# Gated linear attention feeding a cosine-gated MLP: the attention output made as token rows and transposed by TensorE or by a DMA, in a new order of units

## The chip, the core and the metric

The kernel runs on one core of a Trainium2 chip. The metric is the device time of one execution in microseconds (us). The engines are named as in the profile: PE is TensorE's matmuls, PEld its weight loads, DVE is VectorE, ACT is ScalarE, POOL is GpSimd, and SP issues the DMAs. A time is the median of a kernel's runs. A span is what one profiled execution shows from its first to its last instruction, and is 1 to 2 us shorter. PSUM is the memory that PE writes its results to.

## The reference

```python
# q, k, v, alpha: [4, 8, 768, 48];  w_in: [384, 2048];  w_out: [2048, 384]
for t in range(S):                                   # attention with a decaying state
    state = alpha[:, :, t, :, None] * state + einsum('bhd,bhe->bhde', k[:, :, t], v[:, :, t])
    y[:, :, t] = einsum('bhd,bhde->bhe', q[:, :, t], state)
x = y.transpose(0, 2, 1, 3).reshape(B * S, H * D)    # 3072 tokens x 384
h = x @ w_in
out = (h * cos(h)) @ w_out
```

## The kernel before

The 3072 tokens go through in 24 chunks of 128. One chunk passes through small units, and each unit has a letter. A string of letters with chunk numbers is the program: each engine executes its units in the order of that string, without looking ahead to a later unit. These units matter here:

| unit | engine | what it does | PSUM it writes |
|---|---|---|---|
| T, then t | PE, then DVE | transposes k and q; t copies them out | g |
| S, then u | PE, then DVE and POOL | the chunk's addition to the state; u adds and scales (DVE's part is called sc) | g |
| A, then m | PE, then DVE | scores; m masks them out of PSUM | big |
| Y, then y | PE, then DVE | attention output; y copies it out | g |
| F, f, p | PE, ACT, DVE | first half of the hidden layer, its cosine, the gating product | big |
| G, g, q | PE, ACT, DVE | the same for the second half | big |
| V and W, then e | PE, then ACT | the two halves of the second matrix; e copies the sum out | o |
| C, N, l, E | PE and ACT | cumulative log decay of two chunks, every second step; needs another ACT table | big |

PSUM pool g has **one** buffer, used by T, S and Y in turn. Each of them must wait until DVE has emptied the one before. So does o, which has one buffer too; big has three.

```python
    def outputs(j):                       # unit Y, before: 128x64 halves of the array
        t = ps.tile([C, 512], FP, tag="g")          # ps = tile_pool(bufs=1)
        # ... mms: per half 10 matmuls (6 of them in a batch's first chunk)
        kt, start, stop, lhsT, rhs = mms[half][i]   # lhsT: 64 columns of v or of the state
        nc.tensor.matmul(t[64 * half : 64 * half + 64, kt * C : (kt + 1) * C],
                         lhsT, rhs, start=start, stop=stop, skip_group_check=True)

    def ev_outputs(j):                    # unit y, before: what it copies is x already transposed
        t = work.tile([C, 3, C], BF, tag="xT")
        nc.vector.tensor_copy(out=t.rearrange("r k t -> r (k t)"), in_=y_ps.pop(j)[:, 0 : 3 * C])
        x_t[j] = t                        # F(j) and G(j) read it

    run(START)                            # the first chunks, in an order of their own
    for s in range(S0, NCH + 2):          # S0 = 4, NCH = 24
        # ... g = (s + 3) // 2; odd = s % 2 == 1; V = s - 2
        run(f"a{s + 7} k{s + 4} v{s + 4}")          # loads
        run(f"o{s + 2} T{s + 1} t{s + 1} F{s} f{s} S{s + 1} u{s + 1} A{s + 1} m{s + 1}")
        run(f"V{V} G{s} g{s} p{s} Y{s + 1} y{s + 1} q{s}")
        if odd: run(f"N{g} l{g + 1}")
        run(f"W{V} e{V}")
        if odd: run(f"C{g} E{g}")
```

## Time and profile before

| | before |
|---|---|
| time | 209.12 us (2 runs, 209.04 and 209.20) |
| PE busy / DVE / ACT / POOL | 95% / 66% / 63% / 38% |
| PE's share of the chain that ended last | 82% |
| one chunk in the steady part | 7.1 us, 7.6 us with C |
| first T of chunk 5 / of chunk 23 / end of the span | 54.1 / 185.8 / 208.2 us |

The timeline of the kernel before on PE, one step. The columns are start and duration in us, then the source line, what it computes, and how many; a bracket at the end would give idle time before the row. L210 is T, L323 is F or G, L249 is S, L227 is A, L347 is V or W, and L304 is Y, of which only the first and the last row are shown:

```profile
127.51 0.38 PE L210 MATMUL t<-ident_bf,khb 128*128 128x128 bf16 x4
127.73 0.39 PE L210 MATMUL t<-ident_bf,qhb 128*128 128x128 bf16 x4
127.96 1.50 PE L323 MATMUL t<-t,w_114 128*128 128x128 bf16 x24
129.30 0.33 PE L249 MATMUL t<-vpb,khb 128*128 128x96 bf16 x4
129.56 0.40 PE L227 MATMUL t<-t 48*128 48x128 bf16 x8
129.89 1.47 PE L347 MATMUL o_new<-w_116,g_new 128*128 128x384 bf16 x8
131.20 1.50 PE L323 MATMUL t<-t,w_114 128*128 128x128 bf16 x24
132.64 0.25 PE L304 MATMUL t<-t,ub 128*64 128x128 bf16 x2
...
133.11 0.28 PE L304 MATMUL t<-t,vpb 128*64 128x128 bf16 x4
133.32 1.47 PE L347 MATMUL o_new<-w_116,g_new 128*128 128x384 bf16 x8
134.63 0.39 PE L210 MATMUL t<-ident_bf,khb 128*128 128x128 bf16 x4
```

There is no bracket: PE never waits. Between the three users of g lie other units. F (1.34 us) separates T from S; A, V and G (3.1 us) separate S from Y; W (1.31 us) separates Y from the next T. DVE empties g in that time. Y itself takes from 132.64 to 133.32, 0.68 us.

### The profile page before, as it was taken

To read this page: it belongs to the slowest core of one execution; us is meant where nothing else is said; L and a number is where in the kernel's file an instruction comes from. 1 tells how busy PE (TensorE), PEld (TensorE's weight loads), DVE (VectorE), ACT (ScalarE), POOL (GpSimd) and SP (SyncE) were. 2 spreads that over 40 slices of the span, in tenths; PEclk is the share of its full clock that TensorE was granted. 3 is DMA by queue.
4 is the path that set the end of the run, shared out by engine and by line. 5 is a ranking of instruction groups with operands and counts; after the bars stand their busy time and mean duration, and the time that the engine had idled before them with its cause. 6 is when DMAs were issued, how large, how long until landed. Compare 5 with 4: busy or idle time off the path is not lost.

```text
span 208.2 us, 6187 instructions
## 1 busy us (share of the span) xinstructions
PE 196.8 (95%) x2645; PEld 149.0 (72%) x2647; DVE 136.7 (66%) x163; ACT 130.4 (63%) x142; POOL 79.6 (38%) x124
## 2 busy tenths in 40 slices
PE   7996869899999999999999999999999999999982
PEld 2343558677787887877878787787878878787851
DVE  7106857799776668487686685766776776777320
ACT  2064594998964955955937839739659558434420
POOL 3005362485570371561730931912804617401000
PEclk9999997999999999999999999999999999999999
DMA  6999999999999377566765955874774461101112
GB/s 139 312 197 319 186 218 360 260 179 199 179 225 191 80 151 157 113 148 123 160 131 93 188 117 106 162 152 97 135 154 94 100 114 43 41 2 39 38 38 77
DMA packets 106204, 30.29 MB, mean 145 GB/s; under 512 B 100288, under 2 KB 105408, under 8 KB 106176
## 3 DMA queue, kind: packets, MB, share of 16 engines
q1 hardware_dynamic: 106176, 29.89, 66.6%
q8 instruction: 20, 0.33, 0.7%
q14 instruction: 8, 0.07, 0.1%
HBM read 25.17 MB, written 4.72 MB: 144 GB/s over the span
## 4 chain that ended last, share of the span: by engine, by line
PE 82%; DVE 6%; DMA 4%; issue 4%; POOL 1%; SPq 1%; ACT 0%; POOLq 0%; DVEq 0%; ACTq 0%
PE o_new L347 32%; PE t L323 29%; PE t L304 8%; PE t L210 5%; DMA t<-in_k_dram 4%; PE t L227 3%; PE t L249 2%; PE cum_new L161 1%; DVE w_114 L121 1%; DVE g_new L338 1%; DVE t L216 1%; DVE qhb L193 1%; PE cum_new L165 1%; DVE t L309 1%; DVE t L236 1%
## 5 line engine op out<-in xcount | busy, mean ns | idle before, releaser
L331 ACT ACTIVATE c_sb<-t,halfpi 128x1024 bf16<-128x1024 f32 x48 | 53.3, 1115 | 41.7 <-PE t L323 41.3
L323 PE MATMUL t<-t,w_114 128*128 128x128 bf16 x1152 | 72.6, 220 | 0.4 <-DVE g_new L338 0.4
L347 PE MATMUL o_new<-w_116,g_new 128*128 128x384 bf16 x384 | 70.2, 327 | 0.6 <-ACT o_sb L363 0.6
L323 PEld LDWEIGHTS <-w_114 128*128 128x128 bf16 x1152 | 67.9, 99 | 3.5 <-issue 0.5
L338 DVE TENSOR_TENSOR g_new<-t,c_sb 128x1024 bf16<-128x1024 f32 x48 | 58.4, 1219 | 15.2 <-ACT c_sb L331 14.7
L191 POOL TENSOR_TENSOR khb<-t,icp_new 128x384 bf16<-128x384 f32 x24 | 25.0, 1041 | 74.8 <-ACT icp_new L179 73.7
L347 PEld LDWEIGHTS <-g_new 128*128 128x128 bf16 x384 | 34.1, 98 | 24.2 <-issue 0.8
L263 POOL TENSOR_TENSOR ub<-sc,Em 128x384 bf16<-128x384 f32 x20 | 17.4, 870 | 33.1 <-DVE sc L261 33.1
L236 DVE TENSOR_TENSOR t<-t,mask_f 128x1024 bf16<-128x1024 f32 x24 | 29.2, 1215 | 0.0
L193 POOL TENSOR_TENSOR qhb<-t,cp_new 128x384 bf16<-128x384 f32 x22 | 22.0, 1000 | 0.0
L216 DVE COPY t<-t 128x1024 bf16<-128x1024 bf16 x24 | 16.5, 687 | 8.1 <-PE t L210 8.1
L309 DVE CAST t<-t 128x384 bf16<-128x384 f32 x24 | 13.3, 554 | 11.4 <-PE t L304 11.3
L363 ACT ACTIVATE o_sb<-o_new 128x384 f32<-128x384 f32 x22 | 10.7, 485 | 15.9 <-PE o_new L347 15.8
L261 DVE TENSOR_TENSOR sc<-t,ub 128x384 f32<-128x384 f32 x20 | 11.1, 557 | 13.8 <-PE t L249 13.8
L370 PE MATMUL w_ps<-warm 128*128 128x512 bf16 x61 | 17.3, 435 | 1.4 <-DVE warm L56 1.2
L331 ACT ACT_TABLE_LOAD x13 | 16.7, 1283 | 0.2
L141 ACT ACT_TABLE_LOAD x13 | 16.7, 1283 | 0.2
L304 PE MATMUL t<-t,vpb 128*64 128x128 bf16 x288 | 15.9, 222 | 0.2 <-DVE t L216 0.2
L179 ACT ACTIVATE icp_new<-cum_new 128x768 f32<-128x768 f32 (+1 forms) x13 | 9.8, 757 | 7.3 <-PE cum_new L165 7.3
L370 PEld LDWEIGHTS <-warm 128*128 128x128 bf16 x63 | 6.5, 109 | 10.4 <-issue 4.5
L304 PE MATMUL t<-t,ub 128*64 128x128 bf16 x160 | 13.0, 227 | 1.0 <-DVE t L216 0.8
L304 PEld LDWEIGHTS <-vpb 128*64 128x64 bf16 x288 | 13.1, 111 | 0.9 <-issue 0.4
(47 smaller groups left out, 152.9 us busy)
## 6 DMA issues: line engine op xcount, KB each, us to landing
a_new<-in_alpha_dram SPq DMA_DIRECT2D x24, 192.0 KB, 3.7
t<-in_v_dram SPq DMA_DIRECT2D x24, 192.0 KB, 4.3
t<-in_k_dram SPq DMA_DIRECT2D x24, 192.0 KB, 4.0
t<-in_q_dram SPq DMA_DIRECT2D x24, 192.0 KB, 4.3
out_dram<-o_sb SPq DMA_DIRECT2D x24, 192.0 KB, 2.0
w1f<-in_moe_w_in_dram SPq DMA_DIRECT2D x2, 1536.0 KB, 7.8
w2f<-in_moe_w_out_dram SPq DMA_DIRECT2D x2, 1536.0 KB, 10.3
```

Source lines behind the costliest of these rows:

```text
L141: nc.scalar.preload_act_table_set("natural_log_exp_and_others")
L191: nc.gpsimd.tensor_tensor(out=khb[:, j % 3, :, 0:D], in0=k_sb, in1=icp.rearrange("s (h d) -> s h d", h=H), op=ALU.mult)
L193: qeng.tensor_tensor(out=qhb[:, j % 3, :, 0:D], in0=q_sb, in1=cp[:, 0:HD].rearrange("s (h d) -> s h d", h=H), op=ALU.mult)
L216: nc.vector.tensor_copy(out=t, in_=qkT_ps.pop(j))
L236: nc.vector.tensor_tensor(out=t.rearrange("s (h t) -> s h t", h=H), in0=A_ps.pop(j).rearrange("s (h t) -> s h t", h=H), in1=mask_f.unsquee ...
L263: eng.tensor_tensor(out=ub[:, j % 3, :, 0:96].rearrange("r p (a e) -> r p a e", a=2), in0=sc.rearrange("r p (a e) -> r p a e", a=2), in1=E ...
L304: nc.tensor.matmul(t[64 * half : 64 * half + 64, kt * C : (kt + 1) * C], lhsT, rhs, start=start, stop=stop, skip_group_check=True)
L323: nc.tensor.matmul(t[:, f], w1[:, kk, ft * C : (ft + 1) * C], x_t[j][:, kk], start=(kk == 0), stop=(kk == 2))
L331: nc.scalar.activation(out=c_sb, in_=h_ps[j, half], func=AF.Sin, bias=halfpi, scale=1.0)
L338: nc.vector.tensor_tensor(out=g_t[j][:, half * HF : (half + 1) * HF], in0=h_ps.pop((j, half)), in1=c_t.pop((j, half)), op=ALU.mult)
L347: nc.tensor.matmul(o_ps[j][:, 0:DM], g_t[j][:, ft], w2[:, ft], start=(f == 0 and (half == 0 or not whole)), stop=(f == HF - 1 and (half == ...
L370: nc.tensor.matmul(w_ps, warm[:, 0:C], warm, start=True, stop=True)
```

## The change

Its intent: Y's products use only 64 columns of the array at a time. With the scores as the stationary operand instead, the output comes out as 128 token rows, and the streamed operand is 48 or 96 columns long, so PE has less to do. The price is that x must then be transposed. Five first chunks do that on PE, the later ones by one DMA each. The units are put in a new order, apparently to leave the DMA time: V and W now lie between Y and F.

```diff
-    VS = 112
+    JD = 5
-    vpb = consts.tile([C, 3, H, VS], BF, tag="vpb")
-    nc.vector.memset(vpb, 0.0)
-    ub = consts.tile([C, 3, NP, C], BF, tag="ub")
+    vpb = consts.tile([C, 3, H, D], BF, tag="vpb")
+    ub = consts.tile([C, 3, NP, 96], BF, tag="ub")
@@ def outputs(j):   (the 20 half-width matmuls are cut)
+        for p in range(NP):
             if not first:
+                nc.tensor.matmul(t[:, p * 96 : (p + 1) * 96], qT[:, (NP + p) * C : (NP + p + 1) * C],
+                                 ub[:, (j - 1) % 3, p], start=True, stop=False, skip_group_check=True)
+            for h in (2 * p, 2 * p + 1):
+                nc.tensor.matmul(t[:, h * D : (h + 1) * D], A_t[j][:, ACOL[h] * C : (ACOL[h] + 1) * C],
+                                 vpb[:, j % 3, h], start=first, stop=True, skip_group_check=True)
@@ def ev_outputs(j):   (the old lines, and the bookkeeping of y_t and x_t, are cut)
+        t = work.tile([C, HD], BF, tag="y_sb")
+        nc.vector.tensor_copy(out=t, in_=y_ps.pop(j)[:, 0:HD])
+        if j >= JD:
+            x = work.tile([C, 3, C], BF, tag="xT", bufs=3)
+            nc.sync.dma_start_transpose(out=x, in_=y_t.pop(j))
+        else:
+            t = ps.tile([C, 3, C], BF, tag="g")
+            for kt in range(3):
+                nc.tensor.transpose(t[:, kt], y_t[j][:, kt * C : (kt + 1) * C], ident_bf)
+            x = work.tile([C, 3, C], BF, tag="xT", bufs=3)
+            nc.vector.tensor_copy(out=x, in_=t)
@@ main loop
-        run(f"o{s + 2} T{s + 1} t{s + 1} F{s} f{s} S{s + 1} u{s + 1} A{s + 1} m{s + 1}")
-        run(f"V{V} G{s} g{s} p{s} Y{s + 1} y{s + 1} q{s}")
-        if odd: run(f"N{g} l{g + 1}")
-        run(f"W{V} e{V}")
-        if odd: run(f"C{g} E{g}")
+        run(f"o{s + 2} T{s + 1} t{s + 1} S{s + 1} u{s + 1} V{V} A{s + 1} m{s + 1} W{V} e{V}")
+        run(f"F{s} f{s} p{s} G{s} g{s} Y{s + 1} y{s + 1} q{s}")
+        if odd: run(f"N{g} l{g + 1} C{g} E{g}")
```

## The prediction

> **What bounds the kernel now.** TensorE. The page gives PE 95% busy, DVE 66%, ACT 63%; the chain of waits is 82% PE. In the timeline of 125 to 140 us PE never stops: one chunk takes 7.1 us, or 7.6 us with the cumulative sums. Its order is T (transposes) 0.45, F (first half of the hidden layer) 1.34, S (state) 0.27, A (scores) 0.33, V 1.31, G 1.4, Y (attention output) 0.68, W 1.31.
>
> The order matters because T, S and Y all write the one PSUM bank "g" (pool of one buffer), which DVE must empty in between. Now each emptying is covered: F lies between T and S, A V G between S and Y, W between Y and T.
>
> **What the change removes.** Y had 20 half-width matmuls in 0.68 us, plus 0.09 us of drain before them (timeline). Afterwards it is 4 matmuls of 96 columns and 8 of 48: an estimate of 0.41 us from the 43 ns that a 96-column matmul of S takes and some 30 ns for a short one. That is some 8 us in all, all of it on PE.
>
> **What it adds and moves.** The new order on PE is T S V A W F G Y (C). Now nothing lies between T and S, nor (but 0.5 us of sums) between Y and the next T. So PE waits for DVE twice per chunk. DVE's order is t, sc, mask, gate p, y, gate q. y stands behind p, which stands behind ACT's cosine f, which stands behind F: a closed loop. From y's start, with the timeline's durations: y 0.55, so T issues at 0.6 and completes at 1.2; t must wait for q (0.46 to 1.59) and ends at 2.27; S issues at 2.33, V ends at 3.8, A at 4.14, W at 5.45, F at 6.8 (complete 6.95); f 7.0 to 8.1; p 8.15 to 9.28; then the next y: about 9.3 us, and up to 0.4 us more on odd steps, where the cosine's table load comes behind W's eviction. Against 7.4 us that is +2.0 us for each of 19 steps: +38 us. Y's saving lies in PE's new idle time and is worth nothing.
>
> The first five chunks add three PE transposes and a second DVE eviction with PE waiting: about 1.2 us each, partly hidden: +4 us. The DMA transpose has from 0.55 to about 5.4 us before F needs it. The Trainium skill ("VectorE: DVE Perf Modes", "The three transpose paths") gives 1309 ns for a 128x128 one; this trace has none. Three of them, or the 2 us landing of an output store, fit narrowly, so I expect little stall in the loop and about 1 us at the last chunk.
>
> **Prediction.** 209 + 38 + 4 + 1 = 252 us, so 253 us, range 240 to 272. Faster by over 2%: 0.03; within 2%: 0.04; slower: 0.93.
>
> **What would show it.** PE busy falling to some 75 to 80%; PE idle before S put down to DVE's t (1.2 us each) and before T put down to DVE's y (0.7 to 1.3 us each); Y in about 0.4 us; a steady period of 9.2 to 9.6 us; no long wait of F for the DMA.
>
> **What would make it wrong.** A transpose landing later than 5 us, which makes F wait and raises the period (260 us and more); a lower PE clock because of its gaps; a startup that absorbs or multiplies the hand-overs.

## More of the kernel before

The granted clock is the share of TensorE's full clock that the profile shows as granted.

From the page of the kernel before, the busy times of the engines, PE's busy tenths in 40 slices of the span, the clock granted to PE in tenths, and the engines' shares of the chain that ended last:

```profile
PE 196.8 (95%) x2645; PEld 149.0 (72%) x2647; DVE 136.7 (66%) x163; ACT 130.4 (63%) x142; POOL 79.6 (38%) x124
PE   7996869899999999999999999999999999999982
PEclk9999997999999999999999999999999999999999
PE 82%; DVE 6%; DMA 4%; issue 4%; POOL 1%; SPq 1%; ACT 0%; POOLq 0%; DVEq 0%; ACTq 0%
```

## The result and the profile after

The changed kernel is correct and takes 274.88 us (2 runs, 273.83 and 275.92). The ratio to before is 1.3154, with a 95% interval of 1.3029 to 1.3279. (A ratio is the mean time of one kernel's fast runs over the mean of the other's in the same rounds, so it is not quite the ratio of the medians.) It is slower, as forecast, but it lies 3 us above the top of the predicted range.

From the page of the changed kernel, the same lines but the chain, which the profile could follow back only for a quarter of the span:

```profile
PE 212.2 (78%) x2484; PEld 150.4 (55%) x2486; DVE 137.8 (51%) x167; ACT 130.5 (48%) x142; POOL 80.2 (29%) x124
PE   8977598869588598598597597597787787786985
PEclk9999979997799799899899899868979979979999
```

PE now has gaps throughout. The clock is new too: before, it dipped once; now it dips again and again.

The waits of PE in the changed kernel (engine and line, what it waited for: us in total, times, longest). L209 is T, L248 is S, L313 is F, L287 is y, L215 is t:

```profile
PE t L209 <- DVE t L287: 22.5, 18, 1.7
PE t L248 <- DVE t L215: 22.1, 20, 1.6
PE t L313 <- DMA x<-t: 1.0, 1, 1.0
```

These are the two hand-overs of bank g that the new order leaves uncovered, and one wait for a transpose. The timeline on PE, two steps (L226 is A, L337 is V or W, L160 and L164 are C; Y's rows before 152.98 and around 162 are left out):

```profile
152.98 0.38 PE L209 MATMUL t<-ident_bf,khb 128*128 128x128 bf16 x4 [1.68 <-DVE t L287]
153.20 0.39 PE L209 MATMUL t<-ident_bf,qhb 128*128 128x128 bf16 x4
154.72 0.50 PE L248 MATMUL t<-vpb,khb 128*128 128x96 bf16 x4 [1.13 <-DVE t L215]
155.02 2.61 PE L337 MATMUL o_new<-w,g_new 128*128 128x384 bf16 x8
157.56 0.40 PE L226 MATMUL t<-t 48*128 48x128 bf16 x8
157.89 1.47 PE L337 MATMUL o_new<-w,g_new 128*128 128x384 bf16 x8
159.20 2.84 PE L313 MATMUL t<-x,w 128*128 128x128 bf16 x48
161.88 0.21 PE L277 MATMUL t<-ub,t 128*128 128x96 bf16 x1
...
162.26 0.32 PE L160 MATMUL cum_new<-lnab,triu_bf 128*128 128x384 bf16 x1
...
163.63 0.38 PE L209 MATMUL t<-ident_bf,khb 128*128 128x128 bf16 x4 [0.71 <-DVE t L287]
163.85 0.39 PE L209 MATMUL t<-ident_bf,qhb 128*128 128x128 bf16 x4
165.37 0.34 PE L248 MATMUL t<-vpb,khb 128*128 128x96 bf16 x4 [1.13 <-DVE t L215]
165.55 1.46 PE L337 MATMUL o_new<-w,g_new 128*128 128x384 bf16 x8
```

Three things are to be read here. Y takes 0.38 us (161.88 to 162.26) instead of 0.68. PE stands still before each T and each S. And V, the same eight matmuls, takes 2.61 us at 155.02 but 1.46 at 165.55.

The timeline on ACT and on DVE in the same stretch shows the closed loop (L321 is the cosine f, then g; L328 is p, then q; L287 is y; L215 is t):

```profile
160.74 1.11 ACT L321 ACTIVATE c_sb<-t,halfpi 128x1024 bf16<-128x1024 f32 x1 [0.85 <-PE t L313]
161.89 1.23 DVE L328 TENSOR_TENSOR g_new<-t,c_sb 128x1024 bf16<-128x1024 f32 x1 [2.67 <-ACT c_sb L321]
163.03 0.55 DVE L287 CAST t<-t 128x384 bf16<-128x384 f32 x1
163.50 1.22 DVE L328 TENSOR_TENSOR g_new<-t,c_sb 128x1024 bf16<-128x1024 f32 x1
164.63 0.68 DVE L215 COPY t<-t 128x1024 bf16<-128x1024 bf16 x1
```

F ends, f runs (160.74), p runs (161.89), y runs (163.03), then T may start (163.63). But t stands behind q (163.50) on DVE and starts only at 164.63. S waits for t (165.37), and V, A, W and the next F wait behind S. So each step of the ring waits for the one before it, and DVE, with four units in it (p, y, q, t), is busy only 51% of the span.

The clock is read from the view of stretches. Its columns are the stretch, its length, the busy times of PE, PEld, DVE, ACT and POOL with their counts, the granted clock, the DMA share and GB/s. The two stretches are the half-clock window around that slow V, and the equally long one ahead of it:

```profile
150.53:153.94 3.41, 1.38 (x28) 1.12 (x25) 2.70 (x3) 1.68 (x2) 0.99 (x3) 1.00 0.00 0
153.94:157.35 3.41, 2.63 (x12) 1.36 (x12) 1.28 (x3) 0.00 (x0) 0.83 (x1) 0.50 0.71 134
```

After 3.41 us in which PE was busy for 1.38 us, PE gets half the clock for the next 3.41 us. No transfer starts in the first stretch. In the second the DMA engines are busy too (0.71), so contention with the loads is a rival for the slow V. Two more stretches of the same trace speak against it: a W at the full clock under more DMA traffic, and a late V with no traffic (a DMA share above 1 counts the whole time of packets that run on past the stretch):

```profile
157.89:159.36 1.47, 1.47 (x15) 0.95 (x12) 1.23 (x1) 0.00 (x0) 0.00 (x0) 1.00 1.26 201
240.30:242.93 2.63, 2.63 (x13) 1.12 (x12) 0.56 (x1) 0.00 (x0) 0.83 (x1) 0.55 0.00 0
```

The eight matmuls take 1.47 us with the traffic and 2.63 us without it; the time goes with the clock.

Where the 63.8 us between the two spans (272.1 - 208.2) came from, by the starts of T:

| stretch | before | after | difference | predicted |
|---|---|---|---|---|
| up to T of chunk 5 | 54.1 | 58.9 | +4.7 | +4 |
| T of chunk 5 to T of chunk 23 (18 steps) | 131.7 | 190.1 | +58.4 | +38 |
| from there to the end | 22.4 | 23.1 | +0.7 | +1 |

The whole miss lies in the steady steps, which take 10.56 us in the mean (190.1 / 18) instead of the 9.4 of the prediction. (The predicted +38 is for 19 steps of +2.0; the table has 18.)

### The profile page after: what moved, and what is told of

Its sections match the earlier page's. It is cut to its first block, busy times and chain, and to the rows that moved or that the text cites. A ratio compares the mean times of both kernels' runs of the same rounds, so it can differ in the third digit from the quotient of the medians.

```text
span 272.1 us, 5908 instructions
## 1 busy us (share of the span) xinstructions
PE 212.2 (78%) x2484; PEld 150.4 (55%) x2486; DVE 137.8 (51%) x167; ACT 130.5 (48%) x142; POOL 80.2 (29%) x124
## 5 line engine op out<-in xcount | busy, mean ns | idle before, releaser
L328 DVE TENSOR_TENSOR g_new<-t,c_sb 128x1024 bf16<-128x1024 f32 x48 | 58.4, 1219 | 61.2 <-ACT c_sb L321 61.1
L337 PE MATMUL o_new<-w,g_new 128*128 128x384 bf16 x384 | 84.7, 375 | 1.1 <-DVE w L120 0.9
L313 PE MATMUL t<-x,w 128*128 128x128 bf16 x1152 | 70.2, 222 | 1.9 <-DMA x<-t 1.0
L313 PEld LDWEIGHTS <-w 128*128 128x128 bf16 x1152 | 67.8, 99 | 5.4 <-issue 1.5
L321 ACT ACTIVATE c_sb<-t,halfpi 128x1024 bf16<-128x1024 f32 x48 | 52.5, 1113 | 19.1 <-PE t L313 19.0
L337 PEld LDWEIGHTS <-g_new 128*128 128x128 bf16 x384 | 39.4, 110 | 30.6 <-issue 13.2
L209 PE MATMUL t<-ident_bf,khb 128*128 128x128 bf16 x96 | 9.2, 218 | 24.6 <-DVE t L287 22.5
L248 PE MATMUL t<-vpb,khb 128*128 128x96 bf16 x96 | 9.6, 234 | 22.8 <-DVE t L215 22.1
L209 PEld LDWEIGHTS <-khb 128*128 128x128 bf16 x96 | 7.1, 96 | 26.9 <-issue 25.3
L248 PEld LDWEIGHTS <-khb 128*128 128x128 bf16 x96 | 5.7, 109 | 27.0 <-DVE t L215 25.5
L360 PE MATMUL w_ps<-warm 128*128 128x512 bf16 x61 | 17.4, 436 | 1.4 <-DVE warm L56 1.2
L215 DVE COPY t<-t 128x1024 bf16<-128x1024 bf16 x24 | 16.4, 682 | 2.9 <-PE t L209 2.9
L287 DVE CAST t<-t 128x384 bf16<-128x384 f32 x24 | 13.2, 549 | 3.0 <-PE t L280 3.0
L194 POOL CAST vpb<-t 128x384 bf16<-128x384 f32 x24 | 13.7, 571 | 0.0
```

What stands on the lines that cost most here:

```text
L215: nc.vector.tensor_copy(out=t, in_=qkT_ps.pop(j))
L248: nc.tensor.matmul(t[:, p * 96 : (p + 1) * 96], khb[:, j % 3, 2 * p : 2 * p + 2].rearrange("s h d -> s (h d)"), vpb[:, j % 3, 2 * p : 2 * ...
L313: nc.tensor.matmul(t[:, f], w1[:, kk, ft * C : (ft + 1) * C], x_t[j][:, kk], start=(kk == 0), stop=(kk == 2))
L321: nc.scalar.activation(out=c_sb, in_=h_ps[j, half], func=AF.Sin, bias=halfpi, scale=1.0)
L328: nc.vector.tensor_tensor(out=g_t[j][:, half * HF : (half + 1) * HF], in0=h_ps.pop((j, half)), in1=c_t.pop((j, half)), op=ALU.mult)
L337: nc.tensor.matmul(o_ps[j][:, 0:DM], g_t[j][:, ft], w2[:, ft], start=(f == 0 and (half == 0 or not whole)), stop=(f == HF - 1 and (half == ...
```

## The experiments

The theory: order alone makes the loss, in two parts. A ring through the single buffer of g sets the period, and the idle time it makes in PE then costs clock. The row form and the DMA transpose are innocent. Its rivals: the row form or its transposes cost the time, or V is slow through contention with the loads, or each wait stands by itself.

### e1: only the new order

The kernel before, column form and all, with the three `run` lines of the change's main loop.

> The kernel before with nothing changed but the order of the units in the main loop (the changed kernel's order). Theory (the order closes a loop PE-DVE-ACT through the one PSUM bank g, and the new form and the DMA transpose are innocent): the attention output's extra 0.4 us lies in PE's idle time, so the loop's period stays at the changed kernel's 10.6 us against 7.3 us before; without the five chunks with PE transposes (4.7 us) and the wait for the last DMA transpose (about 1 us) some 268 us, 262 to 274. Rival (the row form with its DMA transposes is what costs): 209 to 216 us.

Measured: 263.27 us (262.18 and 264.36), ratio 1.261 (1.2439 to 1.2781). The order by itself makes 54 of the 66 us. Its PE waits the same way: 21.3 us before S and 16.3 before T. It comes out 5 us below the figure expected, within the range: Y, 0.3 us longer, fills some of PE's idle time (1.37 us before a T where the changed kernel has 1.68), and fewer windows are at half clock, 34 us in all instead of the changed kernel's 44. One step shows what such a window costs: from T of chunk 14 to T of chunk 15 none falls, and the step takes 9.38 us, where the like step before it, from T of chunk 12, takes 10.65. The rival falls.

### e2: only the new form

The changed kernel with the loop's order of before.

> The changed kernel with only the loop's order put back to the order before. Theory: the loop through bank g is open again; what is left is that the first hidden half F comes only W and T (1.8 us, 2.3 us with the sums) after the attention output, while the eviction and the DMA transpose take about 3.1 us from there, so PE waits 0.8 to 1.4 us for the DMA in each step: a period of some 8.0 us, 222 to 233 us in all, and the granted clock stays near 1.0 because the gaps are short. Rival (the row form with its DMA transposes is what costs): about 265 to 275 us.

Measured: 234.22 us (233.28 and 235.17), ratio 1.1219, 1 us above the range. Here PE waits for the transposes instead. The wait, and how long a transpose takes from issue to landing, in the same run:

```profile
PE t L313 <- DMA x<-t: 23.9, 19, 2.5
DMA to landing us min/median/max: 2.3/2.3/3.6
```

So the form is not free in the old order: all 19 transposes are waited for. The loss is 25 us against the changed kernel's 66. The theory's mechanism holds, with one step missed: on ACT the cosine f stands behind C's exponentials and a table load (there the load ends at 146.23 us and f starts at 146.25, though its F ends at 145.02), so p is late, and y stands behind p. So in every second step the transpose is issued later than reckoned. The new order did cure this wait (23.9 us became 1.0), and paid for it with two others of 22 us each and the clock.

### e3: dummy matmuls in PE's gaps

```diff
-        run(f"o{s + 2} T{s + 1} t{s + 1} S{s + 1} ...")
+        run(f"o{s + 2} T{s + 1} w{4 if s + 1 < NCH else -1} t{s + 1} S{s + 1} ...")
+        # at the end of the step
+        if s + 1 < NCH: run("w2" if odd else "w6")
```

> The changed kernel with dummy matmuls (512 columns, operands of zero) in PE's two gaps of each step: 4 after the transposes T, and before the next T 6 in even steps, 2 in odd ones; their sum of 0.4 to 1.3 us is shorter than each gap. Theory (on top of the loop of 9.35 and 9.84 us, every second step runs its V at half clock because PE was idle for most of 3.4 us before it): the half-clock stretches vanish, V takes 1.3 us in every step, the loop's mean period falls from 10.56 to 9.6 us, 257 us in all (253 to 261). Rival (V is slow because the loads of that time contend with it): no change, 272 to 277 us.

Measured: 257.22 us (257.46 and 256.99). From T of chunk 5 to T of chunk 23 it takes 173.8 us, after a first step of 10.60 alternately 9.38 and 9.84 us; not one half-clock window is left there. More work on PE makes the kernel 17.7 us faster. The timeline on PE (L360 is the dummy work; its operands are zero, and it still counts as activity):

```profile
145.94 0.38 PE L209 MATMUL t<-ident_bf,khb 128*128 128x128 bf16 x4 [0.38 <-DVE t L287]
146.16 0.39 PE L209 MATMUL t<-ident_bf,qhb 128*128 128x128 bf16 x4
146.38 1.03 PE L360 MATMUL w_ps<-warm 128*128 128x512 bf16 x4
147.67 0.34 PE L248 MATMUL t<-vpb,khb 128*128 128x96 bf16 x4 [0.26 <-DVE t L215]
147.85 1.46 PE L337 MATMUL o_new<-w,g_new 128*128 128x384 bf16 x8
```

The gaps are filled, but not wholly (PE still waits 8.7 us before T and 5.0 before S in all), so the dummies do not set the period; the ring is untouched, and V takes 1.46 us. The rival, contention with the loads, falls: the loads are all still there, and the step of 9.38 us is the one that e1 shows without any dummies. This splits the +58.4 us of the steady part into +42.1 us (173.8 - 131.7) for the ring and +16.3 us (190.1 - 173.8) for the clock, by one profiled run of each.

### e4: V between T and S

```diff
-  T{s + 1} t{s + 1} S{s + 1} u{s + 1} V{V} A{s + 1} ...
+  T{s + 1} t{s + 1} V{V} S{s + 1} u{s + 1} A{s + 1} ...
```

> The changed kernel with one unit moved: V between T and S, so that S's wait for the eviction of T is covered. Theory (one closed loop y, q, t, S, V, A, W, F, f, p sets the period): V leaves the loop, which shortens by V's 1.3 us less what was left of S: periods of about 8.0 and 8.4 us, and with the shorter gap the half-clock stretches go too: about 231 us (226 to 240). Rival (each wait stands by itself: only the 1.1 us gap before S is won, and the half-clock stretches stay): 274 - 18 x 1.1 = 254 us.

Measured: 232.49 us (232.05 and 232.93), ratio 1.1136. Most steady steps take 8.08 and 8.54 us. Moving one unit takes 42 us away, because it takes V out of the ring and, with one gap fewer, no steady window is at half clock any more. Against e3, whose steady part is at full clock too, it is 24.7 us less, near the 1.3 us of V in each of 18 steps. PE still waits 22.0 us before T. The rival, in which only the wait before S is won, falls.

### e5, e6, e7: an order that covers every hand-over

PE: V T W A S F G Y, then C. V lies between Y and T, W between T and S, F and G between S and Y.

```diff
+        run(f"o{s + 2} V{V} T{s + 1} t{s + 1} W{V} A{s + 1} S{s + 1} m{s + 1} F{s} f{s} u{s + 1}")
+        run(f"G{s} e{V} g{s} p{s} Y{s + 1} y{s + 1}")
+        if odd: run(f"C{g}")
+        run(f"q{s}")
+        if odd: run(f"N{g} l{g + 1} E{g}")
```

e5 is the changed kernel with it. e6 also makes the first five chunks in the column form of before, so that they need no transpose (`if j < JD:` the old matmuls and the old y, with the old padded vpb and ub). e7 is the kernel before with this order and nothing else.

> The changed kernel with a third order: on PE V T W A S F G Y C, on ACT W's eviction between the two cosines, on DVE t, mask, sc, p, y, q. Each emptying of bank g is covered again (V between Y and T, W between T and S, F and G between S and Y), and between Y and the next F lie V T W A S, some 3.6 us, more than the 3.1 us that eviction and DMA transpose take. Theory (order alone was the loss, the row form is a gain of some 0.35 us of PE per chunk): a period of 6.7 us, 7.3 with sums, mean 7.05 against 7.31 before; with the 4.7 us of the first five chunks some 209.5 us (206 to 214). Rival (the DMA transpose keeps costing, or each gap is a new one): 220 us and more.

> The kernel of the third order, but the first five chunks in the column form of before, which needs no transpose. Theory (their two hand-overs PE-DVE-PE-DVE cost the 4.7 us of the start): 4.7 us less than the third order alone, about 205 us (202 to 208), faster than before by 1 to 3%. Rival (the start is bound elsewhere): no more than 1 us less.

> The kernel before with the third order and nothing else. Theory (PE was already without gaps, so an order alone cannot win anything, and the gain of the hybrid is the shorter attention output): 209 us within 1% (207.5 to 211). Rival (the third order is itself the gain): 205 us or less.

Measured: e5 214.70 us (4 runs, ratio 1.028, 1.0219 to 1.0341); e6 210.88 us (4 runs, one of them slow, ratio of the fast ones 1.0067, 1.0005 to 1.0130); e7 209.70 us (4 runs, ratio 1.0009, 0.9946 to 1.0073).

The order alone turns 274.9 us into 214.7. The PE transposes of the first five chunks cost 3.8 us (e5 - e6), near the 4.7 us by which the changed kernel reached chunk 5 late. But e5 lies 0.7 us above its range, and e6, expected at 205 and at most 208, gains nothing on before. The reckoning that went wrong is the DMA transpose. The wait, and issue to landing, in e6 (L342 is F):

```profile
PE t L342 <- DMA x<-t: 5.4, 7, 1.2
DMA to landing us min/median/max: 2.3/2.4/3.7
```

Most transposes land in 2.3 us, but now and then one takes over 3 us, and then the 3.6 us between Y and F, less y's wait behind p, are too few. Why some are slow was not settled; the page counts their packets on the same queue as those of the loads and the stores.

### e8: DMA transposes in the first five chunks too

`JD = 0` in the changed kernel.

> The changed kernel with the DMA transpose in the first five chunks too (JD = 0). Theory (the start is where the 16 DMA engines are full, 9 tenths and more, so there the transposes land late and SP, which issues in order, holds back loads behind a transpose that waits for DVE): transposes of the start land in 4 us and more, 276 to 295 us. Rival (PE transposes are the worse in the start too): 4 us less than the changed kernel, 268 to 272 us.

Measured: 279.47 us in the fast run (the profiled one, 286.66, was slow, so only what it shows of the start, before chunk 5, is used). It is slower by about 5 us, as the theory said, but not for the reason it gave first: those five transposes land in 2.3 to 3.2 us, as elsewhere. What happens is that PE waits 13.9 us for them in four waits, and that SP, which issues in order, holds the loads behind a transpose until DVE has made its input: the loads of w_out are issued at 35.5 us instead of 28.4, right after a transpose before which SP had issued nothing for 5 us. By this one fast run, five chunks on PE were the better choice within the change.

### e9, e10: the second hidden half one step later

PE: V T W A S, then G of the chunk before, F, Y, C. Some 5 us of work now lie between a Y and the F that needs its transpose.

```diff
+        L = s - 1 if s > S0 else -1
+        run(f"o{s + 2} V{V} T{s + 1} t{s + 1} W{V} A{s + 1} m{s + 1} S{s + 1} u{s + 1}")
+        run(f"G{L} g{L} e{V} q{L} F{s} f{s} Y{s + 1} y{s + 1} p{s}")
+        if odd: run(f"C{g} N{g} l{g + 1} E{g}")
```

e9 is e6 with it; e10 is the kernel before with it, with a third buffer for x.

> The hybrid with the second hidden half G one step later (PE: V T W A S G of the last chunk, F, Y, C), so that between Y and the F that needs its transpose lie V T W A S G, some 5 us instead of 3.6. In the hybrid PE waited 5.4 us for transposes that landed in up to 3.6 us instead of 2.3. Theory (that wait is what ate the gain of the shorter attention output): no wait of F for the DMA, periods of 6.7 to 6.9 and 7.2 us, from T of chunk 5 to T of chunk 23 125 to 128 us instead of 131.7, and 204.5 us in all (202 to 207). Rival (the gain is not there at all): 208 to 211 us, as the hybrid.

> Control: the kernel before with this order and a third buffer for x, nothing else. Theory (before is bound by PE's work, not by its order): 208 to 210.5 us. Rival (the lagged order is the gain): as the lagged hybrid, 207 us or less.

Measured: e9 205.58 us (6 fast runs, 204.78 to 206.65), ratio 0.9853 (0.9807 to 0.9898). e10 211.78 us (6 runs), ratio 1.0138 (1.0096 to 1.0180), 1.3 us above its range but far from the rival's 207. Of F's waits for a transpose one is left in e9:

```profile
PE t L342 <- DMA x<-t: 0.5, 1, 0.5
```

The steady part takes 126.3 us (54.20 to 180.53) instead of 131.7. e9 is the fastest kernel, 1.5% ahead of before, and the control says what made it so. In the same order the column form takes 6.2 us more (211.78 - 205.58). Between the profiled runs it is 7.5 us: 4.2 of them lie in the steady part (130.57 - 126.33), where only the form of Y differs, so the gain there is the row form's, which needed an order that hides both the hand-overs of g and the transpose. Another 2.3 us lie before T of chunk 5, where both kernels run the same units in the column form, so they are no gain of the row form (e10's run has a half-clock window at 31.0 us, e9's has none there); 0.9 us lie in the end. e10 is 1.4% slower than before although its steady part is not: its T of chunk 5, which now stands behind V, comes 2.4 us later (56.5), and its end takes 1.0 us more (23.4).

## Why the prediction was right or wrong

The direction and the mechanism were right; the size was too small, 253 us against 274.9, just outside the range.

- **What bounds before**: right. e7 shows that a different order without gaps changes nothing (ratio 1.0009).
- **Y in 0.41 us**: right, 0.38 us. Part of the gain may be a drain. The Trainium skill ("TensorEngine Tiling (Array Packing)", "Key Properties") says that changing the tiling mode drains the engine, and the trace fits this, though no run isolates it. Before, 24 matmuls of G from 131.20 at 56 ns each would be done at 132.54, but Y starts at 132.64; after, 48 of them from 159.20 are done at 161.88, where Y starts. That Y's saving is worth nothing in the new order was right too: e1, with the longer Y, is the faster of the two.
- **The ring and its period**: right. 9.3 us and up to 9.7 were predicted; with the clock restored (e3) the steps take 9.38 and 9.84 us. This term came to +42.1 us in 18 steps against the +38 predicted for 19.
- **PE waits before S and T**: right before S (1.13 us, predicted 1.2). Before T they are 0.71 to 0.88 and 1.68 us in turn (predicted 0.7 to 1.3), so the longer one was forecast too small.
- **The start and the end**: right, +4.7 and +0.7 us for +4 and +1.
- **The DMA transpose**: right for the changed kernel. It lands in 2.3 us and is waited for once, 1.0 us. The Trainium skill ("VectorE: DVE Perf Modes", "The three transpose paths") gives 1309 ns for 128x128, and three of those in turn would be 3.9 us, an estimate from that figure; this 128x384 took less than that in the median, and up to 3.7 us at worst.
- **The clock**: this step failed. The prediction named "a lower PE clock because of its gaps" only among the things that could go wrong, and gave it 0 us. Its sum took V at some 1.3 us in every step, where in every second one V takes about 2.6 us; so it forecast a period of 9.2 to 9.6 us, and 10.56 was measured. The clock cost 16.3 us (e3), which is most of the 22 us missed; the ring's other 4 us are nearly all of the rest. The prediction had the waits of 1.2 and of 0.7 to 1.3 us in hand, with only T's 0.45 us between them, and did not ask what PE's activity in one stretch of 3.4 us would be.

## What to carry to other kernels

Where units share a single PSUM buffer, write down for each pair of neighbours what other work of that engine lies between them: when nothing does, the evicting engine's whole queue enters a ring with the bottleneck, although it may be only half busy. A faster form of one unit can be a gain only in an order that hides its new latency; test the form and the order apart, each against a control in the other's setting. And when a change puts gaps into PE, add up PE's busy time over a few us, since short gaps in a row can cost a second time through the clock; dummy matmuls that fit the gaps show that share within one run.

## What the Trainium skill lacked or had wrong

- "TensorE: Matmul & The Clock Gate" (Part 1, and "Why this matters for your kernels") says that the clock falls to half after an idle window of about 3.4 us and advises against PE gaps of more than about 3 us. The trace agrees on the window (half-clock stretches of 3.41 us) and on the factor (0.50), but the advice is not enough: in the changed kernel's steady part no gap of PE is longer than 1.7 us. (The page's section "A second HAM failure mode: psum-queue depth-cycling" does tell of a clock that oscillates from frequent short idle times, but gives no length or share for them.) In the changed kernel's steady part each half-clock window that follows a full-clock one comes after a window in which PE was busy for 1.06 to 1.57 of 3.41 us, by the profile's busy times; in e1 windows of 0.92 to 1.70 us went before, while one of 1.71 us, and in e4 several of 1.73 to 1.75 us, were followed by the full clock. So activity in the window counts, with a boundary near one half in these steady parts, not complete idleness. It is not a rule for more than them: in the start a window of 1.91 us (changed kernel) and one of 1.86 us (e3) were followed by half the clock, and of two half-clock windows of the changed kernel with 2.62 and 2.63 us of PE, the one (174.42) was followed by half the clock again and the other (153.94) by the full clock.
- No page told of a loop that settles on a whole number of windows: the changed kernel's two steps of 9.84 and 10.65 us add up to 20.49 us, six such windows (6 x 3.41 = 20.5), so the same V falls into a half-clock window again and again. That the slow V lengthens the step until it fits is an inference; the longer step of the pair does go from 10.79 over 10.73, 10.69 and 10.66 to 10.65 us, but no run varied it.
- "VectorE: DVE Perf Modes" ("The three transpose paths") has a 128x128 DMA transpose of 1309 ns only. Here one of 128x384, SBUF to SBUF and between loads and stores, took 2.3 us from issue to landing in the median and up to 4.5 us (e5), and kept SP's queue for 1.19 us in the median, in which SP issued no load.
